# The front of an attention and two-layer kernel: v's rows ahead of w_in's words, queries as quarters, a fixed order of products

## The chip, the cores and the metric

One core of a Trainium2 chip runs the whole kernel. The metric is the device time in microseconds (us) of one execution; the median of several runs counts. The profile was taken from one further execution.

## What is computed

Two batches of attention over 768 tokens with 8 heads of 64, each query seeing a window of 16 tokens to either side and 24 block summaries (the maximum of k and the mean of v over blocks of 32 tokens); then a layer of 512 to 1024 to 512 with a softmax gate and a normalisation, then one of 512 to 2048 to 512. Cut to what matters here:

```python
k_sum = k.reshape(B, H, nb, block, D).max(axis=3)
v_sum = v.reshape(B, H, nb, block, D).mean(axis=3)
scores_l = scale * np.matmul(q, k.transpose(0, 1, 3, 2))      # masked to the window
scores_s = scale * np.einsum('bhsd,bhnd->bhsn', q, k_sum) + np.log(block)
a = softmax(np.concatenate([scores_l_masked, scores_s], axis=-1))
x = np.matmul(a, np.concatenate([v, v_sum], axis=2))
h = x @ w_in                                                  # first layer, then its gate and normalisation
y = ln @ w_out
out = elu(y @ w_in2) @ w_out2                                 # second layer
```

## The kernel before

**Tiles and stages.** Attention works on units n of 64 queries (12 a batch, 24 in all), all 8 heads at once. `attn_s(n)` copies the window of k and the block maxima into one of four buffers kw (GpSimd), multiplies the unit's queries by it into PSUM (the scores, L218), and takes the softmax: maximum and mask on VectorE (L224), exponentials on ScalarE (L227), the division on GpSimd (L232). `attn_p(n)` transposes the result (L237) and copies it to pT on ScalarE (L239). `attn_x(j)` multiplies two units by v (L254) into 128 rows of x, transposed, and splits them into an upper and a lower part for exact products (ScalarE L138, VectorE L105). The dense layers run on 128 rows j at a time in three products each (L108 to L110): `mm_in(j, n)` needs xT of j and the four tiles of half n of w_in.

**Words.** The weights arrive as 64-bit numbers. A tile of w_in's words is 512 KB. `convert` makes two parts of it, in a chain over ScalarE (L126), GpSimd (L129), VectorE (L130, L134), ScalarE (L138) and VectorE (L105). There are eight such tiles: four for each half n. The words wait in six buffers.

**Means.** `sum_v(b)` loads v's rows of a batch (six loads of 256 KB), multiplies them by the matrix avg (L188) into PSUM, and copies the means to vsum on ScalarE; `attn_x` of the first units of a batch copies them on GpSimd into the last rows of the four v buffers vw. k and v of a batch stand in two buffers of one kind: `load_k(1)` takes the place of the rows of `sum_v(1)`.

**Order.** All loads are issued by SP, in the order in which the program is written; each may wait for a semaphore of its eight or for its buffer, and what stands behind it on SP waits too. The other engines' order is laid out ahead of the run by a planner that follows the order of the program where its estimate of readiness allows. Before the first data is there, TensorE runs 32 products of zeros (L467, the dummies). The front is written out by hand: the calls from `load_k(0)` to the last `more()` are its order, `more()` being load and conversion of the next tile of w_in. After that a loop over ticks (j, n) calls, in each tick, the loads, the scores, x, the dense product and the transposes that are due; at tick 0 `sum_v(1)`, at tick 1 `load_k(1)` ahead of the tick's loads of v and queries.

The main loads and their sizes, by their shapes: k four of 400 KB, a query 256 KB, mask 180 KB, v's rows for the means six of 256 KB, avg 76 KB, identity 64 KB, v for a unit 192 KB, a tile of words 512 KB.

## Time and profile before

| | us |
|---|---|
| median of three runs (lowest to highest) | 479.31 (479.19 to 480.6) |
| the profiled execution | 480.82 |
| its span, first to last instruction | 479.1 |
| TensorE busy in it | 464.6 |

The profile names TensorE's products PE, its weight loads PEld, VectorE DVE, ScalarE ACT, GpSimd POOL and SyncE's queue SPq. A row of the timeline gives start, length, engine, line, operation, what is written from what, and in brackets the idle time of the engine before it with what ended that. L218 is line 218 of the kernel before. The chain of waits is followed back from the last instruction: at each step to what released it. A load has the time from issue to landing.

### The profile page before, as it was taken

To read this page: it belongs to the slowest core of one execution; us is meant where nothing else is said; L and a number is where in the kernel's file an instruction comes from. 1 tells how busy PE (TensorE), PEld (TensorE's weight loads), DVE (VectorE), ACT (ScalarE), POOL (GpSimd) and SP (SyncE) were. 2 spreads that over 40 slices of the span, in tenths; PEclk is the share of its full clock that TensorE was granted. 3 is DMA by queue.
4 is the path that set the end of the run, shared out by engine and by line. 5 is a ranking of instruction groups with operands and counts; after the bars stand their busy time and mean duration, and the time that the engine had idled before them with its cause. 6 is when DMAs were issued, how large, how long until landed. Compare 5 with 4: busy or idle time off the path is not lost.

```text
span 479.1 us, 7419 instructions
## 1 busy us (share of the span) xinstructions
PE 464.6 (97%) x2603; PEld 390.5 (82%) x2603; DVE 298.6 (62%) x665; ACT 287.0 (60%) x647; POOL 122.1 (25%) x213
## 2 busy tenths in 40 slices
PE   8789999899999999999999999999999999999996
PEld 3466888789988989999888888888888888888885
DVE  3687779885569429786998893367665565450001
ACT  1686697986568428576857673567667656560001
POOL 2797276755443512332222200000000000000000
PEclk9999999999999999999999999999999999999999
DMA  8996994462280543388789514452212212378112
GB/s 280 346 352 212 293 314 162 127 192 79 84 260 16 166 133 128 123 301 318 229 292 367 210 56 137 171 175 58 75 49 84 88 55 77 131 298 275 44 44 88
DMA packets 40116, 82.46 MB, mean 172 GB/s; under 512 B 9616, under 2 KB 18448, under 8 KB 40080
## 3 DMA queue, kind: packets, MB, share of 16 engines
q1 hardware_dynamic: 39936, 81.87, 51.8%
q8 instruction: 20, 0.33, 0.3%
q14 instruction: 16, 0.13, 0.1%
q10 hardware_dynamic: 144, 0.13, 0.1%
HBM read 70.46 MB, written 11.53 MB: 171 GB/s over the span
## 4 chain that ended last, share of the span: by engine, by line
PE 86%; DMA 8%; DVE 3%; ACT 1%; SPq 1%; issue 0%; DVEq 0%
PE o_ps L109 9%; PE o_ps L108 9%; PE o_ps L110 9%; PE h L110 7%; PE h L109 7%; PE h L108 7%; PE c L110 5%; PE c L109 5%; PE c L108 5%; DMA q_bd<-in_qd 5%; PE y_ps L108 5%; PE y_ps L110 5%; PE y_ps L109 5%; PE s_ps L218 3%; PE t_ps L299 2%; DMA vw<-in_v 2%
## 5 line engine op out<-in xcount | busy, mean ns | idle before, releaser
L129 POOL TENSOR_SCALAR conv<-conv 128x512 f32<-128x512 f32 x48 | 38.0, 794 | 81.4 <-ACT conv L126 79.8
L232 POOL TENSOR_SCALAR sm<-sm,st 128x120 f32<-128x120 f32 x96 | 43.5, 471 | 30.5 <-DVE st L230 14.4
L108 PE MATMUL o_ps<-w4r,g_hl 128*128 128x512 f32 x128 | 49.8, 389 | 0.0
L109 PE MATMUL o_ps<-w4r,g_hl 128*128 128x512 f32 x128 | 49.8, 389 | 0.0
L110 PE MATMUL o_ps<-w4r,g_hl 128*128 128x512 f32 x128 | 46.7, 389 | 0.0
L108 PE MATMUL y_ps<-lnT,w_out 128*128 128x384 f32 x128 | 43.6, 341 | 0.8 <-ACT y L316 0.8
L227 ACT ACTIVATE sm<-sm,st 128x120 f32<-128x120 f32 x96 | 36.9, 391 | 10.5 <-DVE st L224 10.5
L109 PE MATMUL y_ps<-lnT,w_out 128*128 128x384 f32 x128 | 43.2, 337 | 0.0
L110 PE MATMUL y_ps<-lnT,w_out 128*128 128x384 f32 x128 | 42.9, 336 | 0.0
L108 PE MATMUL h<-w_in,xT 128*128 128x512 f32 x96 | 39.3, 411 | 0.8 <-ACT xT L138 0.8
L110 PE MATMUL h<-w_in,xT 128*128 128x512 f32 x96 | 38.5, 401 | 0.9 <-DVE xT L105 0.9
L109 PE MATMUL h<-w_in,xT 128*128 128x512 f32 x96 | 38.4, 400 | 0.0
L593 ACT ACTIVATE y<-y 128x512 f32<-128x512 f32 x48 | 30.1, 628 | 0.7
L224 DVE CUSTOM_DVE_ANT_0 sm<-s_ps,mask 128x120 f32<-128x120 f32 x96 | 21.6, 277 | 14.0 <-PE s_ps L218 13.8
L612 DVE COPY y<-o_ps 128x512 f32<-128x512 f32 x5 | 3.5, 690 | 42.9 <-PE o_ps L110 42.9
L218 PE MATMUL s_ps<-kw,q_bd 128*128 128x120 f32 x192 | 25.9, 278 | 4.1 <-DMA q_bd<-in_qd 2.0
L105 DVE TENSOR_TENSOR g_hl<-y,g_hl 128x512 fp32r<-128x512 f32 x32 | 22.4, 702 | 11.5 <-ACT g_hl L138 11.4
L218 PEld LDWEIGHTS s_ps<-kw,q_bd 128*128 128x128 f32 x192 | 23.9, 191 | 7.0 <-POOL kw L101 2.1
L126 ACT ACTIVATE conv<-y 128x512 f32<-128x512 f32 x30 | 20.1, 674 | 14.0 <-DMA y<-in_w_in 12.3
L109 PEld LDWEIGHTS o_ps<-w4r,g_hl 128*128 128x128 f32 x128 | 24.1, 188 | 5.0
L108 PEld LDWEIGHTS o_ps<-w4r,g_hl 128*128 128x128 f32 x128 | 24.0, 188 | 5.0
L110 PEld LDWEIGHTS o_ps<-w4r,g_hl 128*128 128x128 f32 x128 | 24.0, 188 | 5.0
(154 smaller groups left out, 1221.1 us busy)
## 6 DMA issues: line engine op xcount, KB each, us to landing
w4r<-w4d SPq DMA_DIRECT2D x38, 512.0 KB, 3.4
y<-in_w_in SPq DMA_DIRECT2D x16, 512.0 KB, 5.5
w4d<-w3f SPq DMA_DIRECT2D x16, 512.0 KB, 3.4
y<-in_w_out SPq DMA_DIRECT2D x14, 512.0 KB, 5.9
q_bd<-in_qd SPq DMA_DIRECT2D x24, 256.0 KB, 7.2
bits<-in_w_out SPq DMA_DIRECT2D x10, 512.0 KB, 4.9
w4l<-w4d SPq DMA_DIRECT2D x10, 512.0 KB, 4.0
vw<-in_v SPq DMA_DIRECT2D x24, 192.0 KB, 6.7
```

The costliest lines, as they stand in the source:

```text
L105: nc.vector.tensor_tensor(out_, x, hi.bitcast(F32), op=ALU.subtract)
L108: nc.tensor.matmul(ps, lhsT=l[0][ls], rhs=r[0][rs], start=first, stop=False, skip_group_check=parts)
L109: nc.tensor.matmul(ps, lhsT=l[0][ls], rhs=r[1][rs], start=False, stop=False, skip_group_check=parts)
L110: nc.tensor.matmul(ps, lhsT=l[1][ls], rhs=r[0][rs], start=False, stop=last, skip_group_check=parts)
L126: first = nc.scalar.activation(x, high.bitcast(F32), AF.Prelu, scale=TO_F32, alpha=SIGN_TO_28)
L129: nc.gpsimd.tensor_scalar(x, x, MOST, LEAST, op0=ALU.min, op1=ALU.max)
L218: nc.tensor.matmul(sps[:, p, 0:KW], lhsT=q_bd[n][:, p, :], rhs=kw[:, p, :], start=True, stop=True)
L224: nc.vector.tensor_tensor_reduce(sm[:, p, :], sps[:, p, 0:KW], mask[:, mi, :], -scale, 3.0e38, op0=ALU.add, op1=ALU.min, accum_out=nm[:, p ...
L227: nc.scalar.activation(sm[:, p, :], sm[:, p, :], AF.Exp, bias=nm[:, p:p + 1], scale=-1.0, accum_out=ss[:, p:p + 1])
L232: nc.gpsimd.tensor_scalar(sm[:, p, :], sm[:, p, :], ri[:, p:p + 1], 1.0, op0=ALU.mult, op1=ALU.mult)
L299: nc.tensor.transpose(tp[:, i, :], es[j][:, k * 128:(k + 1) * 128], ident)
L593: nc.scalar.activation(m, m, AF.Exp, scale=-1.0)
```

## The change

All rows of v for the first means are now loaded, in three loads of 512 KB with two rows of v to a partition, right behind k, query 0, mask and query 1; avg follows in two halves fitted to that layout, and only then the first tile of w_in's words. Loading and conversion of w_in are separate calls (`words_w_in`, `convert_w_in`), so that the order of loads is written by itself. Queries stand in four fixed tiles whose zero quarters are set once by VectorE; from query 2 on only the two filled quarters are loaded, in two loads. The products of the front have a fixed order on TensorE: scores 0 and 1, the means, transposes 0, scores 2, transposes 1, scores 3, the x products of units 0 and 1, and six more dummies (`keep_busy(6)`). The first conversion is held until the maxima and exponentials of unit 1 are issued. The means of batch 0 go straight into the v buffers 0 (ScalarE) and 1 (VectorE), without GpSimd's copies. At tick 1 `load_k(1)` stands behind the tick's loads.

```diff
--- before.py
+++ after.py
@@ -38,6 +38,7 @@
 NKW = 4
 NV = 4
 NCOPY = 12
+NQ = 4
 NG = 4
 
 
@@ -94,6 +95,12 @@
     kws = [p_at.tile([128, NP, KW], F32, name=f"kw{i}", bufs=1) for i in range(NKW)]
     vws = [p_at.tile([128, DM], F32, name=f"vw{i}", bufs=1) for i in range(NV)]
     avg = p_at.tile([128, 128 + NB], F32, name="avg", bufs=1)
+    qs = [p_at.tile([128, NP, 2 * TQ], F32, name=f"q_bd{i}", bufs=1) for i in range(NQ)]
+    zero = ln_t[:, 4, 0:256].bitcast(BF16)
+    nc.vector.memset(ln_t[:, 4, 0:256], 0.0)
+    for t in qs[2:] + qs[:2]:
+        for hh in range(2):
+            nc.vector.memset(t[hh * D:(hh + 1) * D, :, (1 - hh) * TQ:(2 - hh) * TQ], 0.0)
     nc.gpsimd.memset(negh, -0.5)
     nc.gpsimd.memset(guard, 1e-12)
 
@@ -151,10 +158,14 @@
 
     early = stage[0] + stage[1] + stage[2]
 
-    def load_w_in(n, k):
+    def words_w_in(i):
+        n, k = divmod(i, KD)
+        load_words(early[i % 6], w_in[k * 128:(k + 1) * 128, n * 512:(n + 1) * 512].bitcast(I32))
+
+    def convert_w_in(i):
+        n, k = divmod(i, KD)
         cs = slice(n * 512, (n + 1) * 512)
-        convert(early[(n * KD + k) % 6], w_in[k * 128:(k + 1) * 128, cs].bitcast(I32),
-                w_in_hl[0][:, k, cs], w_in_hl[1][:, k, cs])
+        convert(early[i % 6], None, w_in_hl[0][:, k, cs], w_in_hl[1][:, k, cs])
 
     def load_w_out(k):
         load_words(early[k % 6], w_out[k * 128:(k + 1) * 128, :].bitcast(I32))
@@ -163,7 +174,7 @@
         convert(early[k % 6], None, *w_out_hl[k], gT[:, k:k + 1], pin=True)
 
 
-    k_sb, q_bd, xT, live, ksum, vsum = {}, {}, {}, {}, {}, {}
+    k_sb, q_bd, xT, live, ksum, vsum, marks = {}, {}, {}, {}, {}, {}, {}
 
     def load_k(b):
         k_sb[b] = p_k.tile([128, NP, S + 2 * PAD], F32, tag="k", name="k_sb", bufs=2)
@@ -179,19 +190,32 @@
 
 
     def sum_v(b):
-        pst = psb.tile([128, DM], F32, tag="b", name="vs_ps")
         v_sb = p_k.tile([128, NP, S + 2 * PAD], F32, tag="k", name="v_sb", bufs=2).rearrange("p a s -> p (a s)")
-        for i in range(S // 128):
-            vt = v_sb[:, i * DM:(i + 1) * DM]
-            nc.sync.dma_start(vt, v[b, PAD + i * 128:PAD + (i + 1) * 128, :])
-            c0 = NB - i * 4
-            nc.tensor.matmul(pst, lhsT=avg[:, c0:c0 + 128], rhs=vt, start=i == 0, stop=i == S // 128 - 1)
-        vsum[b] = p_at.tile([128, DM], F32, tag="vsum", name="vsum", bufs=1)
-        nc.scalar.activation(vsum[b][WIN:KW, :], pst[WIN:KW, :], AF.Copy)
+        vts = [v_sb[:, i * 2 * DM:(i + 1) * 2 * DM].rearrange("p (s d) -> p s d", s=2) for i in range(S // 256)]
+        for i, vt in enumerate(vts):
+            nc.sync.dma_start(vt, v[b, PAD + i * 256:PAD + (i + 1) * 256, :].rearrange("(p s) d -> p s d", s=2))
+
+        def products():
+            pst = psb.tile([128, DM], F32, tag="b", name="vs_ps")
+            for i, vt in enumerate(vts):
+                c0 = NB - i * 8
+                for s in range(2):
+                    nc.tensor.matmul(pst, lhsT=avg[:, c0:c0 + 128], rhs=vt[:, s], start=i + s == 0,
+                                     stop=i == S // 256 - 1 and s == 1)
+            vsum[b] = p_at.tile([128, DM], F32, tag="vsum", name="vsum", bufs=1) if b else vws[0]
+            nc.scalar.activation(vsum[b][WIN:KW, :], pst[WIN:KW, :], AF.Copy)
+            if b == 0:
+                nc.vector.tensor_copy(vws[1][WIN:KW, :], pst[WIN:KW, :])
+        return products
 
     def load_q(n):
-        q_bd[n] = p_at.tile([128, NP, 2 * TQ], F32, tag="q", name="q_bd", bufs=4)
-        nc.sync.dma_start(q_bd[n], qd[n])
+        q_bd[n] = qs[n % NQ]
+        if n < 2:
+            nc.sync.dma_start(q_bd[n], qd[n])
+            return
+        for hh in range(2):
+            ds, cs = slice(hh * D, (hh + 1) * D), slice(hh * TQ, (hh + 1) * TQ)
+            nc.sync.dma_start(q_bd[n][ds, :, cs], qd[n, ds, :, cs])
 
     def load_v(n):
         b, t = divmod(n, NT)
@@ -215,22 +239,24 @@
             copy_pool(kw[:, :, 0:WIN], k_sb[b][:, :, t * TQ:t * TQ + WIN])
         sps = psb.tile([128, NP, 128], F32, tag="b", name="s_ps")
         for p in range(NP):
-            nc.tensor.matmul(sps[:, p, 0:KW], lhsT=q_bd[n][:, p, :], rhs=kw[:, p, :], start=True, stop=True)
+            last = nc.tensor.matmul(sps[:, p, 0:KW], lhsT=q_bd[n][:, p, :], rhs=kw[:, p, :], start=True, stop=True)
         sm = p_at.tile([128, NP, KW], F32, tag="sm", name="sm", bufs=NBUF)
         st = p_at.tile([128, 4, NP], F32, tag="st", name="st", bufs=NBUF)
         nm, ss, ri = (st[:, i, :] for i in range(3))
         mi = 1 if t == 0 else (2 if t == NT - 1 else 0)
         for p in range(NP):
-            nc.vector.tensor_tensor_reduce(sm[:, p, :], sps[:, p, 0:KW], mask[:, mi, :], -scale, 3.0e38,
+            marks[n, "max"] = nc.vector.tensor_tensor_reduce(sm[:, p, :], sps[:, p, 0:KW], mask[:, mi, :], -scale, 3.0e38,
                                            op0=ALU.add, op1=ALU.min, accum_out=nm[:, p:p + 1])
         for p in range(NP):
-            nc.scalar.activation(sm[:, p, :], sm[:, p, :], AF.Exp, bias=nm[:, p:p + 1], scale=-1.0,
+            marks[n, "exp"] = nc.scalar.activation(sm[:, p, :], sm[:, p, :], AF.Exp, bias=nm[:, p:p + 1], scale=-1.0,
                                  accum_out=ss[:, p:p + 1])
         nc.vector.tensor_scalar(ri, ss, 1e-9, None, op0=ALU.add)
         nc.vector.reciprocal(ri, ri)
         for p in range(NP):
             nc.gpsimd.tensor_scalar(sm[:, p, :], sm[:, p, :], ri[:, p:p + 1], 1.0, op0=ALU.mult, op1=ALU.mult)
         live[n] = sm
+        return last
+
     def attn_p(n):
         pps = psb.tile([128, NP, 128], F32, tag="b", name="p_ps")
         for p in range(NP):
@@ -245,7 +271,7 @@
         for half in (1, 0):
             n = 2 * j + half
             b, t = divmod(n, NT)
-            if t < NV:
+            if (b or t > 1) and t < NV:
                 copy_pool(vws[n % NV][WIN:KW, :], vsum[b][WIN:KW, :])
         todo_x = [(half, p, hh) for half in (1, 0) for p in range(NP) for hh in range(2)]
 
@@ -258,10 +284,11 @@
         first = product_x(*todo_x[0])
         with tc.issue_after(first.ins), tc.high_priority():
             for args in todo_x[1:]:
-                product_x(*args)
+                last = product_x(*args)
         for half in range(2):
             live.pop(2 * j + half)
         split(*xT[j], xps)
+        return last
 
 
     hs, es = {}, {}
@@ -436,14 +463,8 @@
         yf["B22"] = form("y1", b22)
 
 
-    conv = [lambda n=n, k=k: load_w_in(n, k) for n in range(2) for k in range(KD)]
     words = [lambda k=k: load_w_out(k) for k in range(KF1)]
     parts = [lambda k=k: convert_w_out(k) for k in range(KF1)]
-
-    def more(n=1):
-        for _ in range(n):
-            if conv:
-                conv.pop(0)()
 
     def mm_in(j, n):
         for k in range(KD):
@@ -460,43 +481,67 @@
         ffn1_tr(j, 1)
 
 
-    zero = ln_t[:, 4, 0:256].bitcast(BF16)
-    nc.vector.memset(ln_t[:, 4, 0:256], 0.0)
     busy = psh.tile([128, F1], F32, tag="h", name="busy")
-    for i in range(32):
-        nc.tensor.matmul(busy[:, 0:512], lhsT=zero[:, 0:128], rhs=zero, start=True, stop=True)
+
+    def keep_busy(n, after=None):
+        with tc.issue_after(after.ins) if after else ExitStack():
+            with tc.high_priority():
+                for i in range(n):
+                    nc.tensor.matmul(busy[:, 0:512], lhsT=zero[:, 0:128], rhs=zero, start=True, stop=True)
+
+    keep_busy(32)
 
     loads = tc.manual_schedule(engines={mybir.EngineType.SP})
     loads.__enter__()
     load_k(0)
+    load_q(0)
+    nc.sync.dma_start(mask, mask_d)
     load_q(1)
+    means = sum_v(0)
+    nc.sync.dma_start(avg[0:64, :], avg_d.rearrange("(r two) c -> r two c", two=2)[:, 0, :])
+    nc.sync.dma_start(avg[64:128, 4:], avg_d.rearrange("(r two) c -> r two c", two=2)[:, 0, :124 + NB])
+    words_w_in(0)
+    nc.sync.dma_start(ident, ident_d)
+    load_q(2)
     load_v(0)
-    nc.sync.dma_start(mask, mask_d)
+    load_q(3)
+    load_v(1)
+    words_w_in(1)
+    words_w_in(2)
+    words_w_in(3)
+    load_v(2)
+    load_v(3)
+    words_w_in(4)
+    words_w_in(5)
+    nc.sync.dma_start(gT, g_ln)
     sum_k(0)
-    nc.sync.dma_start(ident, ident_d)
-    load_q(0)
-    more()
-    nc.sync.dma_start(avg, avg_d)
+    first = tc.manual_schedule(engines={mybir.EngineType.PE})
+    first.__enter__()
     attn_s(0)
-    more()
     attn_s(1)
-    sum_v(0)
-    more(2)
+    means()
+    with tc.issue_after(marks[1, "max"].ins), tc.issue_after(marks[1, "exp"].ins):
+        convert_w_in(0)
     attn_p(0)
+    attn_s(2)
     attn_p(1)
-    attn_s(2)
-    load_v(1)
+    attn_s(3)
     attn_x(0)
-    nc.sync.dma_start(gT, g_ln)
-    attn_s(3)
-    load_v(2)
+    keep_busy(6)
+    first.__exit__(None, None, None)
+    convert_w_in(1)
+    convert_w_in(2)
+    convert_w_in(3)
     attn_p(2)
+    words_w_in(6)
     attn_s(5)
-    more(3)
+    convert_w_in(4)
+    convert_w_in(5)
+    convert_w_in(6)
     attn_p(3)
+    words_w_in(7)
     attn_s(4)
-    load_v(3)
-    more()
+    convert_w_in(7)
 
 
 
@@ -515,9 +560,7 @@
     for t, (j, n) in enumerate(ticks):
         s_n, p_n, x_n = t + LEAD, t + LEAD - 2, t + LEAD - 3
         if t == 0:
-            sum_v(1)
-        elif t == 1:
-            load_k(1)
+            sum_v(1)()
         elif t == 3:
             sum_k(1)
         if t % 2:
@@ -529,6 +572,8 @@
                 if u < NU and u not in q_bd:
                     load_q(u)
             load_kw(s_n + 1)
+            if t == 1:
+                load_k(1)
             attn_s(s_n)
         if x_n < NU and x_n % 2:
             attn_x(x_n // 2)
```

## Rows read from the trace of the kernel before

**Rows 1.** The page: busy time of each engine (share of the span) x instructions.

```profile
PE 464.6 (97%) x2603; PEld 390.5 (82%) x2603; DVE 298.6 (62%) x665; ACT 287.0 (60%) x647; POOL 122.1 (25%) x213
```

**Rows 2.** Stages: length; each engine's busy us; granted clock (PEclk), DMA share, GB/s.

```profile
12.00:17.00 5.00, 3.18 (x19) 2.54 (x20) 2.95 (x20) 3.45 (x16) 2.65 (x7) 1.00 1.04 392
...
22.00:28.00 6.00, 3.68 (x50) 3.14 (x50) 5.36 (x23) 4.84 (x16) 4.98 (x8) 1.00 1.05 328
...
28.00:34.00 6.00, 5.66 (x36) 4.64 (x36) 4.54 (x16) 5.11 (x18) 5.49 (x11) 1.00 1.04 335
...
34.00:40.00 6.00, 5.83 (x18) 2.91 (x16) 5.19 (x19) 4.63 (x15) 5.84 (x9) 1.00 0.57 211
```

**Rows 3.** TensorE's waits, 0 to 60 us: us in total, times, longest.

```profile
PE s_ps L218 <- DMA q_bd<-in_qd: 1.7, 2, 1.5
...
PE h L110 <- DVE xT L105: 0.9, 2, 0.6
```

**Rows 4.** Timeline: start, us, engine, line, operation, xcount [idle before <-releaser].

```profile
0.85 0.27 DVE L464 MEMSET ln<- 128x256 f32 x1 [0.85 <-PEq L784]
...
1.17 9.58 PE L467 MATMUL busy<-ln 128*128 128x512 bf16 x32 [1.17 <-DVE ln L464]
...
6.27 3.99 PEld L467 LDWEIGHTS <-ln 128*128 128x128 bf16 x19 [0.28 <-issue]
...
9.52 0.95 DVE L176 TENSOR_REDUCE kw<-k_sb 128x24 f32<-128x768 f32 x1 [0.37 <-DMA k_sb<-in_kT]
...
12.35 2.02 PE L218 MATMUL s_ps<-kw,q_bd 128*128 128x120 f32 x16 [1.59 <-POOL kw L101]
...
13.55 0.69 ACT L126 ACTIVATE conv<-y 128x512 f32<-128x512 f32 x1 [11.54 <-DMA y<-in_w_in]
...
15.83 1.95 PE L188 MATMUL vs_ps<-v_sb,avg 128*128 128x512 f32 x4 [1.47 <-DMA v_sb<-in_v]
...
18.92 2.74 PE L188 MATMUL vs_ps<-v_sb,avg 128*128 128x512 f32 x6
...
22.85 0.66 ACT L126 ACTIVATE conv<-y 128x512 f32<-128x512 f32 x1
...
27.89 0.50 PE L108 MATMUL h<-w_in,xT 128*128 128x512 f32 x1 [0.83 <-ACT xT L138]
...
30.65 0.69 DVE L105 TENSOR_TENSOR w_in<-conv,w_in 128x512 fp32r<-128x512 f32 x1 [0.85 <-ACT w_in L138]
...
41.49 1.15 PE L254 MATMUL x_ps<-pT,vw 120*64 120x64 f32 x32
```

**Rows 5.** Chain of waits, 10 to 62 us: start, us, what.

```profile
15.71 7.70 DMA q_bd<-in_qd
...
40.47 0.33 SPq L171
```

**Rows 6.** DMA traffic from 9.5 to 16 us.

```profile
DMA packets 1186, 2.46 MB, mean 379 GB/s; under 512 B 133, under 2 KB 293, under 8 KB 1186
```

**Rows 7.** Query 0's load, issued at 5.43: from issue to landing.

```profile
DMA to landing us min/median/max: 6.8/6.8/6.8
```

**Rows 8.** Groups by line, 12 to 46 us: busy us, mean ns, idle before.

```profile
L227 ACT ACTIVATE sm<-sm,st 128x120 f32<-128x120 f32 x28 | 10.7, 385 | 1.1 <-DVE st L224 1.1
...
L134 DVE SCALAR_TENSOR_TENSOR conv<-y,conv 128x512 int32<-128x512 int32 x7 | 5.4, 777 | 0.2
```

**Rows 9.** Fifth tile of w_in's words, issued at 20.51: issue to landing.

```profile
DMA to landing us min/median/max: 7.2/7.2/7.2
```

**Rows 10.** Scores, 55 to 62 us: TensorE's idle time, by what ended it.

```profile
  DMA q_bd<-in_qd: 0.6, 2
```

**Rows 11.** A load of kw, issued at 101.24: from issue to landing.

```profile
DMA to landing us min/median/max: 4.6/4.6/4.6
```

**Rows 12.** The query load ahead of it, issued at 100.77: issue to landing.

```profile
DMA to landing us min/median/max: 4.5/4.5/4.5
```

**Rows 13.** Timeline around 88 us.

```profile
87.78 0.65 PE L237 MATMUL p_ps<-ident,sm 128*120 128x128 f32 x4 [0.80 <-DVE st L224]
```

## The prediction

> **What bounds the kernel now.** I read the page's busy times first: TensorE is busy 97% of the span [rows 1]. A change of order can therefore only win what the other 14.5 us hold, so the list of stages comes second: TensorE is busy 3.18 of 5 us from 12 on, 3.68 of 6 from 22 on, and nearly full from 28 on; the DMA share is at 1.0 until 34, and VectorE and ScalarE rise from some 3 of 5 us to some 5 of 6 [rows 2]. The list of waits names who ended TensorE's idle time: loads of queries, 1.7 us, and the lower half of xT, 0.9 in two waits [rows 3]. The timeline gives the places: scores 0 and 1 start at 12.35 after 1.59 us of nothing, the means at 15.83 after 1.47 (v's rows), the first dense product (h, L108) at 27.89 after 0.83 (xT's upper half) [rows 4]. The chain of waits says why: it runs through a query issued at 15.71 that lands 7.70 us later, and again through the load of k for batch 1, which SP issues only at 40.47, when the second means are over [rows 5]. So the front is bound by the order of landings; from 28 on TensorE is the bound, with ScalarE and VectorE close behind.
>
> **The change part by part.** *Order of landings.* While the queue is full it moves 379 GB/s [rows 6]: 1.38 us for a tile of w_in's words (512 KB), and I take loads to land in the order of issue. k stands first before and after; its last piece is there at 9.5, when the last reduce starts [rows 4]. Query 0 stood ninth: issued at 5.43, landed 6.8 us later, at 12.2 [rows 7]. That, and not the GpSimd copy that the row names, is what the scores at 12.35 waited for. Now it stands fifth and lands near 10.2. Scores 0 can start when the last reduce (9.52 + 0.95 = 10.47) and the 32 dummies (1.17 + 9.58 = 10.75) are over [rows 4], 1.6 us earlier. But the means gain nothing from that: v's 1.5 MB and then avg land ahead of them. By their shapes k, two queries, mask, v's rows and avg are 4.0 MB, just what stood ahead of and with v's first piece before; the means began on that piece at 15.83 [rows 4], and will begin near 15.8 again, with all their rows there. Six passes take 2.74 us [rows 4], twelve 5.3: done at 21.1.
>
> *Fixed order of products.* Behind the means now stand, in written order, transposes 0, scores 2, transposes 1, scores 3, the x products and six dummies. Two scores took 2.02 us, x 1.15 [rows 4]; a transpose is half a score. That is 0.5 + 1.0 + 0.5 + 1.0 + 1.1 = 4.1, less 0.3 of overlapping ends; the dummies are 3.99 / 18.6 = 0.215 us each [rows 4], 1.3. Queries 2 and 3 land near 18 and hold nothing any more. If ScalarE copies transposes 1 at once, x ends at 24.9 and h starts at 26.2. If the four exponentials of scores 2 (0.39 each [rows 8]) go ahead of that copy, x waits some 1.2 us and h starts at 27.4. The trace of before doesn't show this order; neither end is nearer, so I take the middle, 26.8. Before, h started at 27.89 and lost 0.3 us more on xT's lower half, the smaller of the two waits in [rows 3]; the dummies cover both waits now, at 1.3 us against 0.8 + 0.3. For the clock they buy nothing that a row shows: it stands at 1.00 in every stage, the ones with idle TensorE too [rows 2]. The term: 28.2 - 26.8 = **1.4 us gained** (0.8 to 2.0).
>
> *Words of w_in behind v.* The first tile landed at 13.5, when ScalarE began on it [rows 4], and the second 1.5 us behind it. Now the first lands at 17.0, the second, with identity, two queries and v's rows between, at 20.6, the third at 21.9, the fourth at 23.2; before, ScalarE was on the fourth at 22.85 [rows 4]. That a tile has landed is not enough: this fourth took from 22.85 to 30.65 + 0.69 = 31.34 [rows 4], 8.5 us, though its ScalarE and VectorE steps are 0.7 to 0.8 each [rows 4, 8]; they queue with the softmax. With the same 8.5 it would be ready at 31.7, 0.4 later than before; with 6, at 29.2. ScalarE and VectorE have only the first tile to do from about 16 to 20.6, and then three tiles and two softmaxes at once, so I also hold 32.1 possible. I take **0.3 us lost** (0 to 0.8). The fifth tile lands at 25.5 instead of 20.51 + 7.2 = 27.7 [rows 9], and those behind it as much earlier. TensorE lost 0.6 us on xT there [rows 3] and some in products stretched among the second means: **0.3 us gained** (0 to 1.2).
>
> *k of batch 1 behind the loads of its tick.* Before, v and queries were queued on SP behind k's issue at 40.47 [rows 5], and TensorE paid 0.6 us in two waits for queries at 57 and 60 [rows 10]. Now those loads go first. **0.5 us gained** (0 to 0.6).
>
> *Queries as quarters.* Half of a later query's bytes go, but it becomes two issues on SP and 512 pieces of 256 bytes. The nearest row is a load of kw, 192 KB in 512 pieces: it lands at 101.24 + 4.6 [rows 11], the query ahead of it at 100.77 + 4.5 [rows 12], 0.6 us apart. A whole query takes 256 KB / 379 GB/s = 0.69 us [rows 6]. So a quartered one takes between 0.4 us (by bytes) and 0.6 (by pieces), a gain of 0.1 to 0.3 us of queue time each and none on the path: zero. The page "DMA: Bandwidth & Descriptors" of the Trainium skill (Specifications; Rules for kernel authors) speaks against this part: under 512 bytes an engine reads, modifies and writes, and two transfers to disjoint halves of the partitions merely follow one another. By that rule, at twice the time by bytes, a query would cost 0.7 us, as much as a whole one, and the sum would stay as it is. The row of kw shows no such doubling for its 384-byte pieces.
>
> *Small edits.* Eight memsets of at most 0.27 us each [rows 4] end by 3.3 us, under the wait for k; SP could wait 0.1 us for the first of them, hidden while k's pieces land. The means straight into two v buffers take two GpSimd copies off and put a VectorE copy on, beside ScalarE's. Zero together; without that cover 0.8 us, as a VectorE step of such width [rows 8].
>
> *Later.* At 87.78 TensorE waits 0.80 us for VectorE [rows 13]. VectorE has no less to do there than before, so an earlier TensorE may wait longer: zero, from 1.0 lost to 0.5 gained.
>
> The sum: 1.4 - 0.3 + 0.3 + 0.5 = 1.9 us off the span of 479.1, leaving 477.2. The profiled execution took 480.82, 1.7 outside its span and 1.5 over the median; nothing outside the span is touched, so I take 1.9 off the median of 479.31: **477.4**. All ends at their worst give 480.3, all at their best 475.0.
>
> **The rivals.** *ScalarE and VectorE become the bound:* h starts earlier, but w_in's tiles are ready when they were, and what the front gains is waited for again. For it: some 15 of 18 us busy on each from 22 to 40 [rows 2], and a second tile that starts 5.6 us later. Against it: TensorE has other scores and the second means to do meanwhile, and the fifth tile comes earlier. Time: 479.3 (478.3 to 480.3).
>
> *Slower:* one mechanism, the fourth tile. TensorE's order behind the dummies is laid out ahead of the run; where its product stands ahead of work that could fill, TensorE waits for the tile. Ready 1.9 us later than before, at 33.2 (landing plus 10), it eats the whole gain; at 35.2 (plus 12, with three tiles and both softmaxes in one queue) the loss is 2.0 net: 481.3.
>
> *More:* ScalarE takes the copy first (h at 26.2), products are no longer stretched, the waits for queries go: 475.4.
>
> *The change does not do what it says:* v's rows ahead of w_in don't start the means earlier, since avg lands last. That is in my sum. It would be otherwise if v's larger rows moved faster than 379 GB/s; three loads could save 1 us at most: 476.4, a part of "more".
>
> **How the numbers follow.** Forecast 477.4 (476.2 to 478.6), chance 0.50; ScalarE and VectorE 0.27; slower 0.11; more 0.12. On this kernel a difference under about 0.3% (1.4 us) can't be told from none. Faster than 477.9 are two thirds of the forecast, all of "more" and a little of the second: 0.49. Slower than 480.7 are the slower case and a tail of the second: 0.12. The rest, 0.39, is the same. The range 475.2 to 480.5 leaves out a part of "more" and most of "slower".
>
> **What would show it.** Right: scores 0 near 10.8, means from 15.8 to 21.1 without a break, h between 26.2 and 27.4 with no wait for xT, no wait for a query behind 20 us. Wrong: means before 15.3; TensorE idle ahead of products over w_in between 28 and 36; longer waits for VectorE around 88; more than 0.7 us of queue time for a quartered query.

## The result, and the profile after

The changed kernel takes **482.81 us** (median of 7 runs, 482.4 to 484.14); the kernel before, on the same chip, 480.6 (7 runs). The ratio of the runs is 1.0061, 95% interval [1.0042, 1.0081] (the quotient of the two medians, 1.0046, lies in it): slower by 0.4 to 0.8%, where 477.4 was forecast. The profiled execution is the slowest of the seven, 484.14, its span 482.4. Line numbers in rows are those of the run's own kernel.

Busy times of the changed kernel, as in [rows 1]: TensorE is busy 2.6 us more, some 1.3 of it in the six dummies.

```profile
PE 467.2 (97%) x2608; PEld 391.2 (81%) x2609; DVE 301.9 (63%) x674; ACT 287.4 (60%) x647; POOL 117.8 (24%) x211
```

The stages, columns as in [rows 2] (the engines are TensorE, its weight loads, VectorE, ScalarE, GpSimd), and a stretch of its own below:

```profile
12.00:17.00 5.00, 2.60 (x4) 1.13 (x5) 1.59 (x13) 3.23 (x15) 3.67 (x10) 0.84 1.01 297
17.00:22.00 5.00, 5.00 (x16) 2.47 (x15) 1.12 (x2) 0.48 (x1) 0.23 (x1) 0.82 0.89 280
22.00:28.00 6.00, 4.75 (x58) 3.60 (x57) 4.80 (x22) 5.95 (x20) 4.49 (x8) 1.00 1.03 299
28.00:34.00 6.00, 3.46 (x17) 2.22 (x17) 4.47 (x9) 4.62 (x11) 5.74 (x10) 1.00 0.98 317
34.00:40.00 6.00, 6.00 (x29) 3.83 (x28) 5.21 (x26) 4.96 (x20) 3.55 (x7) 1.00 0.93 265
...
15.40:18.80 3.40, 3.40 (x6) 1.34 (x5) 1.12 (x2) 0.66 (x1) 1.74 (x5) 0.50 0.91 237
```

Three things differ from [rows 2]. From 17 to 22 VectorE, ScalarE and GpSimd do next to nothing (1.12, 0.48 and 0.23 us), then ScalarE is full (5.95 of 6). From 28 to 34 TensorE is busy 3.46 us instead of 5.66. And the granted clock stands at 0.5 (1.2 GHz) from 15.4 to 18.8; in the kernel before it was 1.00 in every stage. This fall is not most of the loss: three of the seven runs have a mean clock of 1.0 and took 482.40 to 482.81 us, the other four 0.995 or 0.996 and 482.81 to 484.14. TensorE's timeline (columns as in [rows 4]) gives the places:

```profile
10.02 1.94 PE L242 MATMUL s_ps<-kw,q_bd 128*128 128x120 f32 x16
14.40 7.08 PE L203 MATMUL vs_ps<-v_sb,avg 128*128 128x512 f32 x12 [2.44 <-DMA avg<-in_avg]
...
24.87 1.15 PE L280 MATMUL x_ps<-pT,vw 120*64 120x64 f32 x32 [0.74 <-ACT pT L265]
26.18 1.24 PE L490 MATMUL busy<-ln 128*128 128x512 bf16 x5 [0.16 <-issue]
27.78 0.33 PE L263 MATMUL p_ps<-ident,sm 128*120 128x128 f32 x1 [0.36 <-POOL sm L256]
29.14 0.50 PE L115 MATMUL h<-w_in,xT 128*128 128x512 f32 x1 [1.03 <-ACT xT L145]
...
30.80 0.50 PE L117 MATMUL h<-w_in,xT 128*128 128x512 f32 x1 [0.60 <-DVE xT L112]
...
33.27 1.12 PE L242 MATMUL s_ps<-kw,q_bd 128*128 128x120 f32 x8 [0.90 <-DMA q_bd<-in_qd]
...
35.95 0.47 PE L115 MATMUL h<-w_in,xT 128*128 128x512 f32 x1
...
200.71 0.45 PE L115 MATMUL y_ps<-lnT,w_out 128*128 128x384 f32 x1 [0.81 <-ACT y L343]
```

Scores 0 and 1 come 2.3 us earlier than in [rows 4], the means wait 2.44 us for avg and run at the halved clock (7.08 us; the second means, at full clock, take 5.31), and the first dense product h starts at 29.14 instead of 27.89. The last line is a point that both kernels pass; before, it reads:

```profile
198.35 0.44 PE L108 MATMUL y_ps<-lnT,w_out 128*128 128x384 f32 x1 [0.82 <-ACT y L316]
```

So 2.4 of the 3.3 us between the two spans are lost by then; the rest lies within what the spans of one kernel differ from run to run. ScalarE's timeline shows why it was empty and then full:

```profile
15.86 0.66 ACT L133 ACTIVATE conv<-y 128x512 f32<-128x512 f32 x1 [1.29 <-DMA y<-in_w_in]
21.52 0.59 ACT L206 ACTIVATE vw<-vs_ps 24x512 f32<-24x512 f32 x1 [5.00 <-PE vs_ps L203]
22.14 0.68 ACT L133 ACTIVATE conv<-y 128x512 f32<-128x512 f32 x1
...
28.49 0.59 ACT L145 ACTIVATE xT<-x_ps 128x512 fp32r<-128x512 f32 x1
```

Its order is fixed: behind the first tile of w_in stands the copy of the means. It waits 5.00 us for them, and the second tile, there at 20.29, stands behind it; xT's copy comes at 28.49, though x ended at 26.0.

Two more readings bear on the prediction. VectorE's last step for the fourth tile of w_in ran at 30.65 in the kernel before [rows 4]; now it comes 4.6 us later, and the tile is ready at 35.94:

```profile
35.25 0.69 DVE L112 TENSOR_TENSOR w_in<-conv,w_in 128x512 fp32r<-128x512 f32 x1
```

TensorE had other work up to 35.95 and so shows no wait for this tile. The chain of waits (as in [rows 5], a piece from 16.72 on) leads to query 5 instead:

```profile
16.72 8.78 DMA y<-in_w_in
25.50 0.02 issue
25.52 7.62 DMA q_bd<-in_qd
33.14 0.14 issue
33.27 1.12 PE s_ps L242 x8
```

The words of the fourth tile land at 25.50. The second half of query 5, eight loads behind them, is issued 0.02 us later (b_quarters, below, shows why it waits for them), lands at 33.14, and scores 5 start. In the kernel before, query 5 was issued ahead of the fifth tile and landed at 26.44; in the written order it stands behind the fifth, sixth and seventh.

### The profile page after: what moved, and what is told of

Read it like the earlier page. It is cut to its first block, busy times and chain, and to the rows that moved or that the text cites. A ratio compares the mean times of both kernels' runs of the same rounds, so it can differ in the third digit from the quotient of the medians.

```text
span 482.4 us, 7460 instructions
## 1 busy us (share of the span) xinstructions
PE 467.2 (97%) x2608; PEld 391.2 (81%) x2609; DVE 301.9 (63%) x674; ACT 287.4 (60%) x647; POOL 117.8 (24%) x211
## 4 chain that ended last, share of the span: by engine, by line
PE 76%; DMA 10%; DVE 9%; issue 2%; ACT 1%; SPq 1%; DVEq 0%; ACTq 0%
PE o_ps L115 8%; PE o_ps L117 8%; PE o_ps L116 8%; PE h L117 6%; PE h L116 6%; PE h L115 6%; PE c L117 5%; PE c L115 5%; PE c L116 5%; PE s_ps L242 3%; PE y_ps L115 2%; PE y_ps L117 2%; PE y_ps L116 2%; PE x_ps L280 2%; DMA y<-in_w_in 2%
## 5 line engine op out<-in xcount | busy, mean ns | idle before, releaser
L136 POOL TENSOR_SCALAR conv<-conv 128x512 f32<-128x512 f32 x48 | 35.1, 733 | 76.5 <-ACT conv L133 75.0
L256 POOL TENSOR_SCALAR sm<-sm,st 128x120 f32<-128x120 f32 x96 | 43.5, 470 | 31.7 <-DVE st L254 18.5
L248 DVE CUSTOM_DVE_ANT_0 sm<-s_ps,mask 128x120 f32<-128x120 f32 x96 | 21.5, 276 | 11.3 <-PE s_ps L242 11.3
L116 PEld LDWEIGHTS o_ps<-w4r,g_hl 128*128 128x128 f32 x128 | 24.1, 188 | 5.0
L242 PEld LDWEIGHTS s_ps<-kw,q_bd 128*128 128x128 f32 x192 | 24.1, 191 | 2.6 <-issue 1.3
L145 ACT ACTIVATE g_hl<-y 128x512 fp32r<-128x512 f32 x32 | 20.1, 628 | 10.2 <-DVE y L639 10.2
```

Source lines behind the costliest of these rows:

```text
L116: nc.tensor.matmul(ps, lhsT=l[0][ls], rhs=r[1][rs], start=False, stop=False, skip_group_check=parts)
L136: nc.gpsimd.tensor_scalar(x, x, MOST, LEAST, op0=ALU.min, op1=ALU.max)
L145: nc.scalar.activation(hi, x, AF.Copy)
L242: last = nc.tensor.matmul(sps[:, p, 0:KW], lhsT=q_bd[n][:, p, :], rhs=kw[:, p, :], start=True, stop=True)
L248: marks[n, "max"] = nc.vector.tensor_tensor_reduce(sm[:, p, :], sps[:, p, 0:KW], mask[:, mi, :], -scale, 3.0e38, op0=ALU.add, op1=ALU.min, ...
L256: nc.gpsimd.tensor_scalar(sm[:, p, :], sm[:, p, :], ri[:, p:p + 1], 1.0, op0=ALU.mult, op1=ALU.mult)
```

## Experiments

Times are medians, the ratio is to the kernel before on the same chip, which took 479.2 to 479.6 in these runs. The changed kernel did not run beside them, so variants of it are compared with it through these ratios. Edits are shortened: `...` marks lines left out, and a bare name (`avg`, `gT`, `ident`) stands for the load of that tile. The theories: A, ScalarE and VectorE get the words of w_in too late and everything that they feed piles up; B, the written order and its six dummies cost the time; C, the clock that falls after the wait for avg; D, the quarters.

### One part alone, in the kernel before

**b_rows_first**: v's rows and avg ahead of the words.

```diff
     load_q(0)
+    means = sum_v(0)          # six loads of rows, products later
+    nc.sync.dma_start(avg, avg_d)
     more()
-    nc.sync.dma_start(avg, avg_d)
```

> The kernel before with one part of the change: all six loads of v's rows and avg are issued ahead of the first words of w_in; scores, transposes and products are laid out as the kernel before does it, queries stay whole, no dummies are added. Theory A (the words of w_in behind v starve ScalarE and VectorE early, and everything that they must split piles up later): 481.5 to 483, as slow as the changed kernel, with idle ScalarE between 16 and 21 us and TensorE waiting for xT or softmax between 24 and 34. Theory B (the written order of products costs the time, the loads alone don't): 479 to 480. Theory C (the granted clock falls after the 2.4 us without work ahead of the means): 480.5 to 482 and a stretch with the clock at 0.5 among the means.

Measured: 483.51, ratio 1.0080 [1.0056, 1.0103]. TensorE's timeline:

```profile
15.49 7.08 PE L191 MATMUL vs_ps<-v_sb,avg 128*128 128x512 f32 x12 [2.34 <-DMA avg<-in_avg]
...
34.49 0.50 PE L108 MATMUL h<-w_in,xT 128*128 128x512 f32 x1 [1.29 <-ACT w_in L138]
```

This part alone costs about as much as the whole change. The trace shows the wait for avg, means at half clock (0.5 from 16.4 to 19.8), and later a wait of 1.29 us for the fifth tile of w_in (the thirteenth product of h).

**b_fixed_order**: TensorE's front in written order.

```diff
+    first = tc.manual_schedule(engines={mybir.EngineType.PE})
...
-    attn_p(0); attn_p(1); attn_s(2); attn_x(0); attn_s(3)
+    attn_p(0); attn_s(2); attn_p(1); attn_s(3); attn_x(0)
```

> The kernel before with TensorE's front in the written order of the changed kernel (scores 0, scores 1, means, transposes 0, scores 2, transposes 1, scores 3, x), loads in the places they had, queries whole, no dummies. Theory B (the written order makes TensorE wait where other work could fill): 481 to 483, with waits for queries 2 and 3 and for softmax ahead of x. Theory A (only the late words cost): 479 to 480, h within 0.5 us of 27.9. A rival for the written order being the good part: 477.5 to 478.5.

Measured: 479.36, 1.0002 [0.9986, 1.0019]. Alone the written order costs nothing that shows, so theory B falls for the kernel before; in the changed kernel the order was not taken back.

**b_quarters**: queries from the third on as two loads into cleared buffers.

```diff
-        nc.sync.dma_start(q_bd[n], qd[n])
+        nc.sync.dma_start(q_bd[n][ds, :, cs], qd[n, ds, :, cs])   # hh in range(2)
```

> The kernel before with one part of the change: queries from the third on as two quarter loads into buffers cleared once, everything else as it was. The prediction counted this at nothing: 479 to 479.6, a quartered query 0.4 to 0.6 us of queue time. A rival by which the small pieces hold up the queue (0.7 us or more for a query): 480 to 481, with later words and later w_in tiles. A rival by which halved bytes bring waits for queries 2, 5 and 4 forward: 478 to 479.

Measured: 481.60, 1.0050 [1.0035, 1.0065]. The prediction had put this at nothing. DMA of this kernel in one stage (columns as in [rows 2]), then the wait and the issues of its SP, its ScalarE and its TensorE:

```profile
22.50:24.50 2.00, 1.24 (x14) 1.16 (x16) 1.68 (x3) 1.19 (x3) 1.84 (x3) 1.00 0.36 93
```

```profile
SPq L205 <- DMA y<-in_w_in: 2.1, 1, 2.1
```

```profile
23.95 1.67 SPq L123 DMA_DIRECT2D y<-in_w_in  x3
...
30.14 0.68 ACT L132 ACTIVATE conv<-y 128x512 f32<-128x512 f32 x1 [1.53 <-DMA y<-in_w_in]
31.61 0.66 ACT L132 ACTIVATE conv<-y 128x512 f32<-128x512 f32 x1 [0.80 <-DMA y<-in_w_in]
32.18 0.61 ACT L144 ACTIVATE w_in<-conv 128x512 fp32r<-128x512 f32 x1
...
32.84 0.50 PE L114 MATMUL h<-w_in,xT 128*128 128x512 f32 x1 [1.24 <-ACT w_in L144]
```

The queue runs nearly dry (share 0.36, 93 GB/s; the kernel before has 1.09 and 260 there) while SP waits 2.1 us with the issue of query 5 (L205). The traces of all kernels show why: SP's loads use eight semaphores in turn, and a load is issued only when the one eight issues ahead of it has landed (before: avg is issued at 8.19, the third piece of k having landed at 8.17; the second tile of words at 9.51, the fourth piece of k at 9.50; v's first rows at 10.24, query 1 at 10.23). In the first 60 us no load of any of the kernels goes out earlier. I call this a place. Two quarters take two of eight places with 64 KB each. So the fifth tile of words is issued at 23.95 instead of 20.51, and ScalarE starts on it at 30.14 instead of 28.88. Behind this step and that of the sixth tile, also late, stands the upper part of the fourth tile, for which TensorE waits 1.24 us.

**b_k1**: k of batch 1 behind its tick's loads.

```diff
-        elif t == 1:
-            load_k(1)
...
             load_kw(s_n + 1)
+            if t == 1:
+                load_k(1)
```

> The kernel before with one part of the change: k of batch 1 is issued behind the loads of its tick instead of ahead of them. The prediction counted 0.5 us gained (0 to 0.6), from two waits for queries at 57 and 60: 478.8 to 479.3 against 479.4. A rival by which the gain passes into the waits for VectorE near 87 and 90: 479.3 to 479.7, with these waits longer by what the others lose.

Measured: 478.43, 0.9983 [0.9971, 0.9996]; the two waits of [rows 10] are gone. The only kernel faster than both.

### Places or small pieces

**b_halves**: two issues for a query, with all bytes, in pieces of 2 KB.

```diff
-        nc.sync.dma_start(q_bd[n], qd[n])
+        for hh in range(2):
+            ds = slice(hh * D, (hh + 1) * D)
+            nc.sync.dma_start(q_bd[n][ds], qd[n, ds])
```

> The kernel before with queries from the third on loaded as two issues of 64 partitions each, with all their bytes in pieces of 2 KB: as many issues as quarters, no small pieces, no saved bytes. If places in the queue are what quarters cost (a load is issued when the one eight issues ahead has landed): 481 to 482.5 as with quarters, the fifth tile of words issued near 23 instead of 20.5 us, a wait for w_in between 30 and 34. If the small pieces cost it: 479 to 479.8, the fifth tile issued by 21.

Measured: 486.65, 1.0150 [1.0113, 1.0187], more than with quarters. The fifth tile is issued at 23.75, and TensorE's timeline reads:

```profile
35.28 1.12 PE L223 MATMUL s_ps<-kw,q_bd 128*128 128x120 f32 x8 [1.74 <-DMA q_bd<-in_qd]
...
37.79 3.75 PE L188 MATMUL vs_ps<-v_sb,avg 128*128 128x512 f32 x4 [1.06 <-DMA v_sb<-in_v]
```

No small piece is left and the loss is larger, above both expectations: the small pieces are not needed for the cost. As with quarters, the fifth tile waits for its place; here the queries also keep all their bytes, and query 4 lands at 35.15 instead of 31.64. The four products of 3.75 us run at half clock. Both kernels load a query by 64 partitions at a time; that was not varied by itself.

**b_quarters_w4**: quarters, with the fifth tile's words right behind query 2.

```diff
     attn_s(2)
+    words_early(4)
     load_v(1)
```

> The kernel before with quartered queries, and the fifth tile of words issued right behind query 2 instead of behind query 5, so that it no longer waits for a place. If places cost: 478.8 to 480 against 481.6 with quarters alone, the fifth tile there by 26, no wait for w_in near 32. If the small pieces cost: 481 to 482 again.

Measured: 483.29, 1.0087 [1.0057, 1.0117]. The tile lands at 24.1, and no product waits for w_in any more. But ScalarE now has the tile's first step ahead of other work and waits 1.05 us for it, and x waits 1.50 for ScalarE. The expectation missed: with that wait gone the time did not come back. So the places are seen to delay the words, but that this delay is the whole price of the quarters is not shown.

**a_q_early2**: the changed kernel, with queries 5 and 4 ahead of the fifth tile.

```diff
-    words_w_in(4); words_w_in(5); gT
...
     attn_s(1)
+    load_q(5)
+    load_q(4)
+    words_w_in(4); words_w_in(5); gT
     means()
```

> The changed kernel with queries 5 and 4 issued ahead of the fifth tile of words, this time behind scores 0 and 1 in the program, so that these still read their own queries (in the run before, the two loads stood ahead of scores 0 and 1, which so used the wrong queries and waited for them). If the wait of 1.07 us for query 5 near 33 is all that is lost there: 481.7 to 482.2 against 482.8. If the wait passes to the words behind (fifth and sixth tile each some 0.9 us later) or to the softmax: 482.5 to 483.2.

Measured: 484.52, 1.0110 [1.0079, 1.0141]. This is above both expectations: query 5 lands at 28.03 instead of 33.14, but its scores now stand earlier and wait 1.62 us for it, and the second means wait 3.06 for their rows. (In a_q_early, 499.53, the two loads stood ahead of scores 0 and 1, which so read the wrong queries; it computes something else, and its time says nothing here.)

### One part taken back, in the changed kernel

**a_no_dummies** and **a_whole_q** (every query whole).

```diff
-    keep_busy(6)
...
-        if n < 2:
+        if n < B * NT:
```

> The changed kernel without the six dummies behind the x products. Theory B (dummies cost): 1.3 us less, 481.5. Theory A: xT, not TensorE, sets the first dense product (29.1, 1.0 us of idle time ahead of it), so nothing changes: 482.8 within 0.5. If the dummies keep the clock up, the granted clock falls after 26 us and the time rises by up to 1 us.

> The changed kernel with every query loaded whole in one load (256 KB) instead of two quarters. Theory D (quarters cost: two issues each on SP's eight semaphores, small pieces, and a query that TensorE waits 0.9 us for at 33.3): 1 to 1.5 us less, 481.5. Theory A: a whole query takes 0.65 us of the queue instead of about 0.45, so the tiles of w_in land 0.4 us later still: 482.8 to 483.3.

Measured: 482.21, 1.0061 [1.0046, 1.0077], and 482.76, 1.0074 [1.0052, 1.0096]: neither helps. Without dummies the wait that they covered stays (1.76 us for softmax instead of 0.36) and the clock falls a second time (0.5 from 29.4 to 32.8): the mean clock of the six runs is 0.988 to 0.993, with dummies it was 0.995 to 1.0. The ratio is the same with and without them, so what they cost and what they keep of the clock seem about equal.

**a_words_first** (the first two tiles of words and avg ahead of v's rows) and **a_loads_back** (the whole front loaded in the order of the kernel before).

```diff
-    means = sum_v(0)
     avg; words_w_in(0); ident
+    words_w_in(1)
+    means = sum_v(0)
...
-    words_w_in(1)
```

> The changed kernel, but v's rows for the means load behind the first two tiles of w_in's words again (avg first, then tile 0, identity, tile 1, then v's rows). Theory A (ScalarE and VectorE starve: with v's rows ahead they have one tile of w_in to convert between 16.5 and 21.5 us, and the rest of the softmax, the copies and xT then pile up behind the means): the second tile lands near 14 instead of 20.3, ScalarE works on through 16 to 22, the first dense product starts 1 to 2 us earlier than 29.1, and the time falls by 1.5 to 3 us to 480 to 481.3. Theory B (the six dummies and the written order of products cost it): no change, 482.8. Theory C (TensorE's clock, halved from 15.4 to 18.8 after the idle 2.4 us ahead of the means): no gain, since the means start no earlier than about 14 either way.

> The changed kernel with one part undone: SP issues the loads of the front in the order of the kernel before (query 1 and v's first piece behind k, the first two tiles of words ahead of v's rows, the others right behind them); the written order of products, the six dummies, quarters, larger rows of v, means straight into v buffers and the later k stay. Theory A (v's rows ahead of the words are the whole loss): 479 to 480.5, within 0.3% of the kernel before. If other parts lose too (dummies 0.6 by their own run, the rest unknown): 481 to 482.5. If the order of loads is not the cause after all: 482.5 to 483.5.

Measured: 485.21, 1.0126 [1.0100, 1.0152], and 484.64, 1.0109 [1.0091, 1.0127]. Both got slower, above every expectation; theory A, as it stood, falls. ScalarE and TensorE of a_loads_back:

```profile
27.81 0.66 ACT L133 ACTIVATE conv<-y 128x512 f32<-128x512 f32 x1 [1.81 <-DMA y<-in_w_in]
...
29.51 0.57 ACT L145 ACTIVATE xT<-x_ps 128x512 fp32r<-128x512 f32 x1
```

```profile
30.14 0.50 PE L115 MATMUL h<-w_in,xT 128*128 128x512 f32 x1 [3.62 <-ACT xT L145]
```

x was ready by 25.1. But in ScalarE's order the fifth tile stands ahead of three exponentials and xT; its issue comes at 22.24 behind the quarters of query 5, it lands at 27.79, and TensorE waits 3.62 us for xT. A late load blocks whatever stands behind its first step.

**a_avg_first** (avg ahead of v's rows) and **a_fill_gap**.

```diff
+    avg
     means = sum_v(0)
-    avg
...
     attn_s(1)
+    keep_busy(12)
     means()
```

> The changed kernel with the two loads of avg ahead of v's rows, nothing else: the means can start on v's first rows (landed at 11.1) instead of 14.4. Theory A (ScalarE and VectorE starve behind the means): the means end 3 to 4 us earlier, the copies and transposes come that much earlier, but the tiles of w_in land as late as before; the first dense product about 1 to 2 us earlier, the time 481 to 482. Theory B (dummies): 482.8, no change. Theory C (clock): no idle time of over 1 us ahead of the means, granted clock 1.00 throughout, about 0.5 to 1.7 us less: 481.1 to 482.3.

> The changed kernel with twelve more dummy products (0.215 us each, some 2.6 us) between scores 1 and the means, which fill the 2.4 us in which TensorE waits for avg. Theory C (the clock that falls after that wait is the loss): the means take 5.3 us instead of 7.1 at a granted clock of 1.0, and the time is 480.5 to 481.5. Theory A (ScalarE and VectorE set the start of what follows, so that faster means gain nothing): 482 to 483.5, the means faster but transposes, x and h no earlier.

Measured: 481.71, 1.0047 [1.0027, 1.0067], and 483.84, 1.0100 [1.0078, 1.0123]. TensorE of a_fill_gap:

```profile
14.89 5.39 PE L203 MATMUL vs_ps<-v_sb,avg 128*128 128x512 f32 x12 [0.22 <-issue]
...
28.32 0.50 PE L115 MATMUL h<-w_in,xT 128*128 128x512 f32 x1 [1.50 <-ACT xT L145]
...
32.17 1.12 PE L242 MATMUL s_ps<-kw,q_bd 128*128 128x120 f32 x8 [1.14 <-DMA q_bd<-in_qd]
```

The means take 5.39 us at full clock, and nothing comes of it: h waits longer for xT. With the three runs of the changed kernel at a clock of 1.0, which were slow too, theory C, the clock among the means as the loss, falls.

### Can TensorE's waits be taken away?

**b_rows_avg** (b_rows_first with avg ahead of the rows) and **c_q2_first** (b_k1 with query 2 ahead of the third tile).

```diff
     sum_v(0)
+    load_q(2)
     more(2)
```

> The kernel before with all of v's rows ahead of the first words, and avg ahead of the rows, so that the means can begin with the first piece of rows instead of behind the last. Rows first with avg last gave 483.5. If the wait for avg and the clock that falls after it are the loss (2.5 us idle, then 1.7 us in products at half clock): 479.5 to 481, a granted clock of 1.0 among the means. If the words that come 3.4 us later are the loss: 482.5 to 483.5 whatever the means do.

> The kernel before with k of batch 1 behind its tick's loads (478.4 alone) and query 2 issued ahead of the third tile of words instead of behind the fourth. Scores 2 waited 1.6 us for this query in the kernel before. If TensorE's waits at the front are worth their length: 477 to 478. If the wait passes to xT and w_in, since ScalarE and VectorE get the third and fourth tile later by 0.7 us: 478.4 to 479.2.

Measured: 485.04, 1.0108 [1.0085, 1.0131], and 482.85, 1.0066 [1.0040, 1.0092], both above their expectations. In b_rows_avg the means run at once, and scores 2 then wait 6.00 us for their query. In c_q2_first the wait for query 2 is gone; ScalarE, TensorE and a stretch read:

```profile
26.64 0.67 ACT L126 ACTIVATE conv<-y 128x512 f32<-128x512 f32 x1 [1.10 <-DMA y<-in_w_in]
...
27.96 0.57 ACT L138 ACTIVATE xT<-x_ps 128x512 fp32r<-128x512 f32 x1
```

```profile
28.59 0.79 PE L108 MATMUL h<-w_in,xT 128*128 128x512 f32 x1 [2.71 <-ACT xT L138]
```

```profile
27.40:34.30 6.90, 5.71 (x19) 4.92 (x20) 4.81 (x17) 5.26 (x20) 5.36 (x11) 0.51 1.04 340
```

The 1.5 us of [rows 3] come back as 2.71 for xT, and the clock falls. x ended at 25.9; as in a_loads_back, xT stands behind the fifth tile in ScalarE's order. In the kernel before it stands ahead of it (xT at 27.26, the tile there at 27.70). This order is laid out ahead of the run, so moving one load in the program also changed what ScalarE waits for first.

**a_avg_whole** (avg first and whole queries, in the changed kernel) and **b_fixed_k1** (b_fixed_order and b_k1 together).

> The changed kernel with two parts undone, avg ahead of v's rows and whole queries. If quarters and the wait for avg are what makes the changed kernel slower and merely cover each other: 479.3 to 480.3, close to the kernel before. If what remains (words behind v's rows, so that ScalarE and VectorE get tiles late and TensorE waits for softmax, xT and w_in) keeps the time: 481 to 482.5.

> The kernel before with the two parts that did no harm alone: the written order of products at the front (1.0002 alone) and k of batch 1 behind its tick's loads (0.9983 alone). If the parts add: 478.3 to 479, faster than both kernels. If the written order takes the gain back: 479.3 to 480.

Measured: 481.02, 1.0031 [1.0014, 1.0048], and 480.11, 1.0015 [1.0001, 1.0029]. TensorE of a_avg_whole, and a stretch of it:

```profile
12.37 5.32 PE L203 MATMUL vs_ps<-v_sb,avg 128*128 128x512 f32 x12
...
25.90 0.47 PE L115 MATMUL h<-w_in,xT 128*128 128x512 f32 x1
...
29.88 0.79 PE L115 MATMUL h<-w_in,xT 128*128 128x512 f32 x1 [0.97 <-ACT w_in L145]
...
31.88 2.03 PE L242 MATMUL s_ps<-kw,q_bd 128*128 128x120 f32 x8 [1.21 <-DMA q_bd<-in_qd]
```

```profile
26.80:37.00 10.20, 8.02 (x28) 6.04 (x27) 6.76 (x19) 5.75 (x17) 4.72 (x8) 0.50 1.04 393
```

Here the front does what the prediction wanted: h at 25.90, 2.0 us earlier than in the kernel before. It is given back at once, in waits for w_in and query 5 and in 10.2 us at half clock; the mean granted clock of its 12 runs lies between 0.989 and 0.996. About half of the loss is recovered, not all. The clock alone could be what is left: an estimate from these rows is that 8.02 us of products at half clock would take some 4 at the full one (eight score products took 2.03 us here, 1.05 at full clock), and this kernel is 1.6 us slower than the kernel before. No run separates the two. b_fixed_k1 doesn't add up either: no wait is left between 40 and 62, but the gain of b_k1 is gone; the trace was not followed further.

## Why the prediction was wrong, step by step

*Front, +1.4: failed, the largest term.* Scores 0 and 1 came as forecast or earlier (10.0 against 10.8). The means ended at 21.5 against 21.1, but by luck: they started 1.4 us early and lost 1.8 to the clock. x ended at 26.0, between the ends that I gave. But h came at 29.14 instead of 26.8, later than before by 1.2. "The dummies cover both waits now" is the step that failed: they end at 27.4, and xT's copy comes at 28.49, behind the exponentials of scores 2 and 3 and a tile's first step, on a ScalarE that has the work of 17 to 22 still to do. "For the clock they buy nothing that a row shows" was the second fault: the rows of before hold no wait as long as the 2.44 us ahead of the means, so they could not show what follows one, and without the dummies the clock was lower in every run (a_no_dummies).

*Words behind v, -0.3, and later tiles, +0.3: failed.* The step at fault is the rate, 379 GB/s. The loads did land in the order of issue, as I took them to, but between 17 and 22 at 280 GB/s: the third tile at 23.7 instead of 21.9, the fourth at 25.5 instead of 23.2, the fifth at 28.4 instead of 25.5. ScalarE began on the fourth tile at 26.80, and it was ready at 35.94 instead of 31.7. These 9.1 us are close to the 8.5 that I took; the start was late. Query 5, behind these tiles, landed at 33.14 and cost 0.90: the sum followed queries 2 and 3 only and had no term for the place of query 5.

*Quarters, 0: failed as a part, about right in its price of queue time.* From the landing of the load ahead to that of its second half, a quartered query took 0.46 to 0.56 us in the first four of the changed kernel, against a forecast of 0.4 to 0.6; a later one took 0.79 (landed at 40.70). A piece of 256 bytes keeps one of the 16 DMA engines busy for 18 ns in the trace, so 512 of them make 0.58 us, 1.7 times the 0.35 by bytes. The page "DMA: Bandwidth & Descriptors" of the Trainium skill (Specifications) says that transfers under 512 bytes are read, modified and written; it puts no factor on that, and the 0.7 us in the prediction, twice the time by bytes, is an estimate above what the pieces took. What was not counted is the place: alone, quarters cost 0.50%. The rows to see it stood in the trace of before, in SP's issues that follow landings by 0.02 us.

*k of batch 1, +0.5: right alone* (0.8 us, interval 0.2 to 1.4), but not kept beside the written order.

*Dummies: right* that 1.3 us are about paid for; taking them away changes nothing. *Later, 0:* the wait of [rows 13] grew from 0.80 to 1.22.

*The rivals.* "ScalarE and VectorE become the bound" named a part of the mechanism, with 479.3 too low: it let the gain at the front be waited for again, no more. The traces show extra cost, since late loads hold up ScalarE's order. "Slower: the fourth tile" priced a tile that is ready at 35.2 with 481.3; in the changed kernel it was ready at 35.94, so its premise came true, though the wait in front of it was for query 5. In b_quarters TensorE does wait for the fourth tile, 1.24 us.

*What is shown and what stays open.* Shown: v's rows first and quarters are each enough to make the kernel before slower; the written order alone is not, and taking the dummies out gains nothing; the half clock among the means does not set the end; two issues for a query cost time without any small piece. Seen in the traces, but not separated by a run: that places are the whole price of the quarters. Open: why the two damages cover each other in the changed kernel (argued only: both end in the same late ScalarE work from 22 to 34 and in the late query 5), and what the last 0.3% of a_avg_whole is: the clock, words behind rows, the late query 5, or the parts that were not tried alone: the larger rows, the means copied straight into v buffers, the held first conversion. No variant of the changed kernel got back to the time before.

## What to carry to other kernels

Before reordering loads, count the places: find from the issues which earlier landing each one waits for, since here a load of 64 KB took a place just as one of 512 KB did. Before crediting an earlier TensorE, follow the in-order engine that feeds it (here ScalarE) instruction by instruction up to the operand wanted; in the runs here that took a wait of TensorE away at the front, the time came back at the next, and only b_k1, which left the front alone, was faster. Parts of a change do not add: measure them alone and together.

## What the runs showed of the hardware

The granted clock fell from 1.0 (2.4 GHz) to 0.5 (1.2 GHz) behind single waits of TensorE of 2.44 us (the changed kernel) and 2.34 (b_rows_first), within waits of 6.00 (b_rows_avg) and 2.71 (c_q2_first), and behind shorter ones in succession (1.74 and 1.06 in b_halves). In the profiled run of a_words_first a wait of 2.46 us ahead of the means was followed by no fall. With the clock at the lower level for 3.4 us of them, the twelve products of the means took 7.08 us instead of 5.3. In a_whole_q a run's time went with its mean clock: 481.3 to 481.8 us at 0.999, 482.4 to 483.1 at 0.996 and 484.4 at 0.993.

The loads of SP landed in the order of issue in the first 60 us of every trace here, and none was issued before the one eight ahead of it had landed. One piece of a load kept a DMA engine busy for 18 ns (256 bytes), 84 ns (2 KB) or 159 ns (4 KB), medians in the changed kernel. Its second, third and fourth tile of words landed 2.2, 3.4 and 1.8 us behind the load ahead of each, against 1.5 for the first and 1.38 at the 379 GB/s of [rows 6]; no run here tells why.
